# Neighbouring PSUM banks for a pair's products, and low parts subtracted by POOL, in a chunked attention with two feed-forward layers

## The chip, the cores and the metric

One Trainium2 chip, of which one core runs the whole program. The metric is the device time of one execution in microseconds. The engines of the core work side by side and each takes its own instructions in order: TensorE (PE for matmuls, PEld for loading weights), VectorE (DVE), ScalarE (ACT), GpSimd (POOL), and SyncE (SP), which here only issues DMAs.

## The reference

Attention in chunks of 64 tokens (4 batches, 8 heads, 576 tokens, head size 64), then two feed-forward layers over the 2304 tokens, with 512 features and 2048 hidden units, all in float32.

```python
scores = scale * np.matmul(q_c, k_c.transpose(0, 1, 2, 4, 3))       # chunks of 64 x 64
attn = softmax(scores)                                              # with 1e-09 in the sum
x = np.matmul(attn, v_c)                                            # -> [2304, 512]
h = x @ moe_w_in;   x = (h - np.tanh(h)) @ moe_w_out
h = x @ moe2_w_in;  x = (h * np.tanh(np.log1p(np.exp(h)))) @ moe2_w_out
```

The second activation is Mish.

## The kernel before

**Split numbers.** Every operand of a large matmul is kept as two rounded halves, a high part (ScalarE copies it with rounding) and a low part (the number minus its high part, a subtraction on VectorE). A product takes three matmuls: high by high, high by low, low by high (`THREE`). The helper `sub` (L80) issues the subtractions, so they all carry line 81, and `add` line 84.

**Layer 1** runs in 80 steps (`steps`): five blocks of tokens (512, 256, 512, 512, 512) by 16 units of 128 hidden features. Step s does `gemm1(s)` (12 matmuls into bank 4 or 5, `hidden`), the activation in pieces on ScalarE and VectorE (`gap_act`, `gap_mid`, `gap_poly`, and a step later `gap_end`), the high part (`hi_part`, ScalarE) and low part (`lo_part`, VectorE) of step s-1, and `gemm2(s-2)` (12 matmuls into banks 0 to 3). After a block's last unit `evacuate` copies banks 0 to 3 out and stores them in DRAM as the input of layer 2. The order in which everything is issued is written out by hand in the loop over `s`.

**Jobs inside layer 1.** From step 35 on, 16 jobs prepare the weights of layer 2, eight of w_in and eight of w_out, spread over the steps by the lists `job` and `cast`. A job loads, unpacks (`j_low`, `j_float`) and forms seven sums of quarter matrices (`j_sums`) in a tile `jf` that has two buffers. For w_out `j_split` makes the halves, `js`: ScalarE writes the high part, ScalarE writes the negated numbers, and a DMA issued by POOL adds the numbers to them (L194 to L200). `j_store` then writes both halves to DRAM; every `js` tile has one buffer. When all jobs are done (step `ends`) their memory is given to layer 2, and the first token pair is loaded (`x_load`), summed (`x_sums`, VectorE) and split (`x_split`, high parts on ScalarE, low parts on VectorE) in the next steps.

**Layer 2** works on three pairs of token blocks (2 x 384 tokens). It uses a scheme with seven products in place of eight quarter products for both matrix multiplications.

- `group1(p, jj)` is the first one, four groups for each pair of token blocks. A group has two neighbouring units, j0 = 2jj and j1 = 2jj+1. `both(p, jj, n)` issues product n (0 to 6) of j1 and then of j0, six matmuls each. Product n goes to bank `BANK1[n]` for j0 and four banks further for j1. Products 4, 5 and 6 go on accumulating in the banks of 0, 2 and 3. `bank1(n)` (L583) is the pair of banks n and n+4, read by one instruction: a copy by ScalarE (L597), sums by VectorE (L84, `u2`, `u3`, `g`), Mish by ScalarE (L587). At a group's end VectorE forms three more sums of `g`.
- The weights of a group come as two parts (`wf_load` on SP's queue, `wf_hi` on ScalarE, `wf_lo` on VectorE), for j1 and j0 each: part 0 for products 0 to 3, part 1 for 4 to 6. `wf_lo` issues the next load into the buffer that it has read. Part 1 has a single buffer for j1 and j0.
- `phase2(p)` is the second one: 56 slots of six matmuls, whose operand `g_split` prepares three slots ahead. Its results lie in neighbouring banks (`bank2`). At the same time the tokens of the next pair are loaded, summed and split.

For the first group the four products 0 to 3 of unit 1 are computed ahead, between layer 1's last gemm1 and its last gemm2s, into banks 4 to 7; those of unit 0 follow when `evacuate` has emptied banks 0 to 3.

Of the kernel before, what the change touches and what calls it, by code (L numbers as in the profile page):

```python
# [46 lines left out]
def attn_moe_moe(ctx, tc, qkv, w1, w2, out):  # L47
# [32 lines left out]
    def sub(o, a, b):  # L80
        nc.vector.tensor_tensor(o, a, b, op=ALU.subtract)  # L81
# [112 lines left out]
    def j_split(n, part):  # L194
        t = JF[n] if part == 0 else JF.pop(n)
        m, src = (4, t[:, 4:]) if part == 0 else (3, t[:, :3])
        o = (SA, SB)[part][n] = pools["j"].tile([P, 2, m, 2 * P], F32R, tag=f"s{part}", name="js", bufs=1)
        nc.scalar.copy(o[:, 0], src)
        nc.scalar.activation(o[:, 1], src, AF.Copy, scale=-1.0)
        nc.gpsimd.dma_start(out=o[:, 1].bitcast(F32), in_=src, accum_op=ALU.add)  # L200
# [193 lines left out]
    def lo_part(s):  # L394
        t = BLOCKS[steps[s][0]]
        sub(GO[s][:, 1, :t], GF.pop(s), GO[s][:, 0, :t].bitcast(F32))
# [87 lines left out]
    for i, n in enumerate(ORD):  # L484
        s = first_job + JOBS[i]
        at(cast, s, (j_turned, n))
        at(job, s, (j_low, n))
        at(job, s + 1, (j_float, n))
        if i + 2 < 2 * NJ:
            at(job, s + 1, (j_load, ORD[i + 2]))  # L490
        at(job, s + 2, (j_sums, n))
        ends = max(ends, s + 3)
        if n >= NJ:
            at(cast, s + 3, (j_split, n, 0))
            at(cast, s + 4, (j_split, n, 1))
            at(job, s + 5, (j_store, n, 0))
            at(job, s + 6, (j_store, n, 1))
            ends = max(ends, s + 6)
# [21 lines left out]
    def x_split(c, part, n):  # L520
# [9 lines left out]
        else:  # L530
            sub(lo, src, hi.bitcast(F32))
# [10 lines left out]
    def wf_load(p, j, part):  # L542
        m, src = ((4, slice(0, 4)), (3, slice(4, 7)))[part]
        pool = pools["x"] if part == 0 and j % 2 else pools["f"]
# [8 lines left out]
    def wf_lo(p, j, part):  # L553
        t = W2[p, j, part]
        sub(t[:, 1], WF.pop((p, j, part)), t[:, 0].bitcast(F32))
        if part == 0 and j + 2 < NJ:
# [9 lines left out]
    BANK1 = (2, 3, 0, 1, 2, 0, 1)  # L566

    def product1(p, j, n):
        a, c = ORDER[n]
        ps = banks[:, BANK1[n] + 4 * (j % 2), :TH]  # L570
# [12 lines left out]
    def bank1(n):  # L583
        return banks[:, n:8:4, :TH]
# [4 lines left out]
    def group1(p, jj):  # L589
        j1, j0 = 2 * jj + 1, 2 * jj  # L590
        g = G[p, jj] = pools["g"].tile([P, 7, 2, TH], F32, tag=f"g{jj}", name=f"g{jj}")
        if p + jj:
            both(p, jj, 0)
        else:
            product1(p, j0, 0)
        u2, u3 = out_tile(), out_tile()
        nc.scalar.copy(u2, bank1(2))  # L597
        if p + jj:
            both(p, jj, 1)
        else:  # L600
            product1(p, j0, 1)
        wf_hi(p, j0, 1)
        add(u2, u2, bank1(3))
        wf_lo(p, j0, 1)
        if p + jj:
            both(p, jj, 2)
        else:
            product1(p, j0, 2)
        add(u3, u2, bank1(0))
        if p + jj:  # L610
            both(p, jj, 3)
        else:
            product1(p, j0, 3)
        W2.pop((p, j0, 0))
        W2.pop((p, j1, 0))
        add(g[:, 3], u3, bank1(1))
        if jj == NJ // 2 - 1:
            w2_load(p, 0)
            w2_load(p, 1)
            mish(g[:, 3], g[:, 3])  # L620
            for k in range(AHEAD - 1):
                g_split(p, k)
        else:
            wf_hi(p, j1 + 2, 0)
            mish(g[:, 3], g[:, 3])
# [4 lines left out]
        mish(g[:, 0], bank1(2))  # L630
        both(p, jj, 5)
        add(g[:, 1], u2, bank1(0))
        mish(g[:, 1], g[:, 1])
# [8 lines left out]
        add(g[:, 2], u2, bank1(1))  # L642
# [3 lines left out]
        add(g[:, 4], g[:, 1], g[:, 3])  # L646
        sub(g[:, 5:7], g[:, 1:5:3], g[:, 0:1].to_broadcast([P, 2, 2, TH]))
        sub(g[:, 1], g[:, 2], g[:, 6])
# [9 lines left out]
    def g_split(p, k):  # L658
        q, j = divmod(k, NJ)
        src = G[p, j // 2][:, (0, 6, 5, 4, 2, 3, 1)[q], j % 2]  # L660
# [78 lines left out]
    for s in range(NS):  # L739
# [40 lines left out]
        if ends + 2 <= s < ends + 6:  # L780
            x_split(s - ends - 2, 0, 0)
            x_split(s - ends - 2, 1, 0)
        if s == NS - 1:
            wf_hi(0, 1, 0)
# [19 lines left out]
        if 0 <= c < 5:  # L804
# [5 lines left out]
            if c < 4:  # L810
                x_sums(c)
    assert not streamed and not job and not cast and ends + 5 < NS
    nc.scalar.preload_act_table_set("mish")

    wf_lo(0, 1, 0)
# [3 lines left out]
    for n in range(4):  # L819
        product1(0, 1, n)  # L820
# [9 lines left out]
    wf_load(0, 0, 0)  # L830
    wf_load(0, 1, 1)
    wf_hi(0, 0, 0)
    wf_lo(0, 0, 0)
# [57 lines left out]
```

## Time and profile before

| | before |
|---|---|
| median of 3 runs | 947.79 us (946.19 to 950.15) |
| the profiled execution | 952.0 us |
| its span, first to last instruction | 950.2 us |
| TensorE matmul / weight load busy | 850.5 / 736.6 us |
| VectorE / ScalarE / POOL busy | 666.6 / 516.4 / 23.2 us |
| mean granted clock of TensorE | 0.966 |

Times in the trace are microseconds from the span's start; 1.8 us of the profiled execution lie outside the span. L575 are the matmuls of `group1`, L674 those of `phase2`, L320 and L329 those of layer 1. "Idle before" is the time in which the engine stood still ahead of an instruction, with what ended it. Layer 1 ends near 514 us; `group1` fills 518 to 605, 664 to 746 and 805 to 886 us, `phase2` the stretches between and the end.

### The profile page before, as it was taken

How to read it: one execution, taken by the hardware profiler on the slowest of the kernel's cores; microseconds unless marked ns; L12 is line 12 of the kernel's file. 1: busy time of each engine (PE TensorE's matmuls, PEld its weight loads, DVE VectorE, ACT ScalarE, POOL GpSimd, SP SyncE). 2: the span in 40 equal slices, each digit the busy share in tenths (PEclk: the TensorE clock that was granted, in tenths of full speed). 3: DMA queues.
4: the chain of work that ended last, by engine and by line, in shares of the span. 5: the costliest groups of instructions: out<-in, count | busy, mean ns of one | idle time of the engine just before them, and what ended most of it. 6: DMA issues, size and time to landing. Idle time of an engine off the chain costs nothing.

```text
span 950.2 us, 13624 instructions
## 1 busy us (share of the span) xinstructions
PE 850.5 (90%) x5244; PEld 736.6 (78%) x5244; DVE 666.6 (70%) x1048; ACT 516.4 (54%) x867; POOL 23.2 (2%) x32
## 2 busy tenths in 40 slices
PE   7889989998899899989895788899888899888898
PEld 6667779976677777767664777899777799777897
DVE  7999758768697889668482555587555686555664
ACT  4888746657557667566353333465333465333443
POOL 0011100000000000000000000000000000000000
PEclk9999999999999999989997799999989999999999
DMA  9945736446898989797813321788221887231774
GB/s 379 419 154 122 166 125 207 158 156 227 290 359 218 348 313 327 229 296 200 281 35 121 100 81 35 270 287 296 95 79 37 290 288 277 94 94 55 250 264 136
DMA packets 60081, 193.83 MB, mean 204 GB/s; under 512 B 4848, under 2 KB 33008, under 8 KB 46832
## 3 DMA queue, kind: packets, MB, share of 16 engines
q1 hardware_dynamic: 56272, 180.37, 54.2%
q0 software_dynamic: 3744, 12.58, 7.1%
q8 instruction: 41, 0.67, 0.3%
q14 instruction: 24, 0.20, 0.1%
HBM read 140.51 MB, written 39.85 MB: 190 GB/s over the span
## 4 chain that ended last, share of the span: by engine, by line
PE 47%; DVE 24%; DMA 13%; ACT 10%; issue 5%; SPq 1%; DVEq 0%; ACTq 0%; POOLq 0%
PE banks L674 17%; PE banks L575 14%; PE banks L329 7%; PE banks L320 7%; DMA wf<-win 3%; DVE g L84 3%; DMA js<-jf 3%; DMA wout<-js 2%; DVE g L365 2%; DVE g L366 2%; DVE w L81 2%; DMA w<-wf 1%; DVE o L84 1%; DVE g L378 1%; DVE t L81 1%
## 5 line engine op out<-in xcount | busy, mean ns | idle before, releaser
L575 PE MATMUL banks<-xo,w 128*128 128x384 f32 x1008 | 212.3, 364 | 48.9 <-DVE o L84 20.5
L575 PEld LDWEIGHTS banks<-xo,w 128*128 128x128 f32 x1008 | 187.0, 203 | 74.2 <-DVE o L84 28.3
L329 PE MATMUL banks<-go,w 128*128 128x512 f32 (+1 forms) x960 | 225.9, 384 | 15.6 <-ACT go L392 5.6
L320 PE MATMUL banks<-x,w 128*128 128x512 f32 (+1 forms) x960 | 216.6, 374 | 7.1 <-DVE w L81 2.6
L329 PEld LDWEIGHTS banks<-go,w 128*128 128x128 f32 x960 | 171.5, 194 | 54.0 <-DVE go L81 7.6
L320 PEld LDWEIGHTS banks<-x,w 128*128 128x128 f32 x960 | 168.4, 189 | 43.4 <-DVE w L81 3.9
L674 PE MATMUL banks<-s,w 128*128 128x384 f32 x1008 | 176.4, 337 | 5.0 <-DVE g L84 3.1
L674 PEld LDWEIGHTS banks<-s,w 128*128 128x128 f32 x1008 | 174.5, 188 | 6.9 <-DVE g L84 4.1
L81 DVE TENSOR_TENSOR s<-g,s 128x384 fp32r<-128x384 f32 x168 | 87.2, 554 | 39.3 <-ACT s L662 39.1
L662 ACT CAST s<-g 128x384 fp32r<-128x384 f32 x168 | 81.7, 511 | 45.1 <-PE banks L674 43.9
L551 ACT CAST w<-wf 128x1024 fp32r<-128x1024 f32 (+1 forms) x48 | 44.7, 934 | 71.2 <-PE banks L575 41.7
L392 ACT CAST go<-g 128x512 fp32r<-128x512 f32 (+1 forms) x80 | 46.2, 578 | 67.4 <-DVE g L366 67.4
L587 ACT ACTIVATE g<-g 128x768 f32<-128x768 f32 x36 | 30.5, 847 | 92.3 <-DVE g L84 92.3
L378 DVE TENSOR_TENSOR g<-z,banks 128x512 f32<-128x512 f32 (+1 forms) x80 | 50.2, 627 | 40.5 <-ACT t L373 40.3
L84 DVE TENSOR_TENSOR g<-o,banks 128x768 f32<-128x768 f32 x36 | 34.4, 954 | 61.9 <-PE banks L575 61.9
L84 DVE TENSOR_TENSOR o<-o,banks 128x768 f32<-128x768 f32 x39 | 37.1, 952 | 54.0 <-PE banks L575 41.2
L81 DVE TENSOR_TENSOR w<-wf,w 128x1024 fp32r<-128x1024 f32 (+1 forms) x54 | 59.4, 1102 | 19.1 <-ACT w L551 18.6
L372 ACT ACTIVATE z<-banks 128x512 f32<-128x512 f32 (+1 forms) x80 | 43.9, 548 | 42.4 <-PE banks L320 42.3
L366 DVE COPY_PREDICATED g<-m,t 128x512 f32<-128x512 int16 (+1 forms) x80 | 55.1, 688 | 2.8
L81 DVE TENSOR_TENSOR go<-g,go 128x512 fp32r<-128x512 f32 (+1 forms) x80 | 50.4, 630 | 4.1 <-ACT go L392 4.1
L365 DVE SCALAR_TENSOR_TENSOR g<-z,g 128x512 f32<-128x512 f32 (+1 forms) x80 | 50.6, 633 | 2.8 <-ACT z L384 2.7
L81 DVE TENSOR_TENSOR t<-banks,t 128x512 f32<-128x512 f32 (+1 forms) x80 | 50.5, 631 | 0.0
(59 smaller groups left out, 663.1 us busy)
## 6 DMA issues: line engine op xcount, KB each, us to landing
w<-wout SPq DMA_DIRECT2D x42, 1024.0 KB, 5.6
w<-w1s SPq DMA_DIRECT2D x21, 1024.0 KB, 7.6
w<-w SPq DMA_DIRECT2D x16, 1024.0 KB, 19.9
jraw<-w SPq DMA_DIRECT2D x16, 1024.0 KB, 7.0
qkv<-qkv SPq DMA_DIRECT2D x18, 768.0 KB, 6.7
wf<-win SPq DMA_DIRECT2D x24, 512.0 KB, 3.8
wf<-win SPq DMA_DIRECT2D x24, 384.0 KB, 3.1
w1s<-w SPq DMA_DIRECT2D x8, 1024.0 KB, 8.8
```

Source lines behind the costliest of these rows:

```text
L81: nc.vector.tensor_tensor(o, a, b, op=ALU.subtract)
L84: nc.vector.tensor_tensor(o, a, b, op=ALU.add)
L320: nc.tensor.matmul(ps, w[:, a, k * P:(k + 1) * P], x[:, c, k, :BLOCKS[b]], start=n == 0, stop=n == 3 * KD - 1)
L329: nc.tensor.matmul(banks[:, m, :t], w[:, a, DM + m * P:DM + (m + 1) * P], g[:, c, :t], start=f == 0 and n == 0, stop=f == NF - 1 and n == 2)
L365: nc.vector.scalar_tensor_tensor(g, z, PK, g, op0=ALU.add, op1=ALU.mult)
L366: nc.vector.copy_predicated(g, m.bitcast(I16), t)
L378: nc.vector.tensor_tensor(g, z, ph, op=ALU.mult)
L392: nc.scalar.copy(o[:, 0, :BLOCKS[steps[s][0]]], GF[s])
L551: nc.scalar.copy(t[:, 0], WF[p, j, part])
L575: nc.tensor.matmul(ps, w[:, x, c % 4, k * P:(k + 1) * P], XO[p][:, a, y, k], start=m == 0 and n < 4, stop=m == 5, skip_group_check=n > 3)
L662: nc.scalar.copy(t[:, 0], src)
L674: nc.tensor.matmul(ps[:, m], w[:, x, j % 4, m * P:(m + 1) * P], s[:, y], start=n == 0 and j == 0 and q < 4, stop=n == 2 and j == NJ - 1, s ...
```

## The change

- **Banks.** `BANK1` is renumbered, and the two units of a pair write neighbouring banks: products 0 and 4 use banks 6 and 7, product 1 banks 4 and 5, products 2 and 5 banks 0 and 1, products 3 and 6 banks 2 and 3. `bank1(n)` is now `banks[:, b:b + 2]`. Two of the rows of `g` change places, so that one sum reads neighbouring rows.
- **Start of layer 2.** Instead of products 0 to 3 of unit 1, products 0 and 1 of both units are computed ahead. For that the first part of unit 0's weights is loaded and converted during layer 1 (step 79), after that of unit 1, which moves two steps ahead (step 77); it uses another pool. The loads for units 2 and 3 move behind that of unit 1's second part.
- **POOL.** `sub` takes an engine, and POOL now subtracts the low parts of layer 1's activation from step 32 on, of all tokens of layer 2 (`x_split`), of the second weight parts (`wf_lo`, part 1), and of the w_out sums. The latter replaces the negated copy on ScalarE and the accumulating DMA.
- **Stores.** `j_store` comes one step earlier, and so does all that follows step `ends`.

```diff
@@ -77,8 +77,8 @@ sub
-    def sub(o, a, b):
-        nc.vector.tensor_tensor(o, a, b, op=ALU.subtract)
+    def sub(o, a, b, eng=None):
+        (eng or nc.vector).tensor_tensor(o, a, b, op=ALU.subtract)
@@ -196,8 +196,7 @@ j_split
-        nc.scalar.activation(o[:, 1], src, AF.Copy, scale=-1.0)
-        nc.gpsimd.dma_start(out=o[:, 1].bitcast(F32), in_=src, accum_op=ALU.add)
+        sub(o[:, 1], src, o[:, 0].bitcast(F32), nc.gpsimd)
@@ -393,7 +392,7 @@ lo_part
-        sub(GO[s][:, 1, :t], GF.pop(s), GO[s][:, 0, :t].bitcast(F32))
+        sub(GO[s][:, 1, :t], GF.pop(s), GO[s][:, 0, :t].bitcast(F32), nc.gpsimd if s >= 2 * NF else nc.vector)
@@ -493,9 +492,9 @@ plan of the jobs
-            at(job, s + 5, (j_store, n, 0))
-            at(job, s + 6, (j_store, n, 1))
-            ends = max(ends, s + 6)
+            at(job, s + 4, (j_store, n, 0))
+            at(job, s + 5, (j_store, n, 1))
+            ends = max(ends, s + 5)
@@ -528,7 +527,7 @@ x_split
-            sub(lo, src, hi.bitcast(F32))
+            sub(lo, src, hi.bitcast(F32), nc.gpsimd)
@@ -541,7 +540,7 @@ wf_load
-        pool = pools["x"] if part == 0 and j % 2 else pools["f"]
+        pool = pools["x"] if part == 0 and (j % 2 or p + j == 0) else pools["f"]
@@ -552,8 +551,11 @@ wf_lo
-        sub(t[:, 1], WF.pop((p, j, part)), t[:, 0].bitcast(F32))
-        if part == 0 and j + 2 < NJ:
+        sub(t[:, 1], WF.pop((p, j, part)), t[:, 0].bitcast(F32), nc.gpsimd if part else nc.vector)
+        if p + j // 2 == 0 and part == 0:
+            if j:
+                wf_load(0, 0, 0)
+        elif part == 0 and j + 2 < NJ:
@@ -563,11 +565,11 @@ product1
-    BANK1 = (2, 3, 0, 1, 2, 0, 1)
+    BANK1 = (6, 4, 0, 2, 6, 0, 2)
...
-        ps = banks[:, BANK1[n] + 4 * (j % 2), :TH]
+        ps = banks[:, BANK1[n] + j % 2, :TH]
@@ -581,7 +583,7 @@ bank1
-        return banks[:, n:8:4, :TH]
+        return banks[:, BANK1[n]:BANK1[n] + 2, :TH]
@@ -589,48 +591,38 @@ group1
+        u2, u3 = out_tile(), out_tile()
...
-        else:
-            product1(p, j0, 0)
-        u2, u3 = out_tile(), out_tile()
-        nc.scalar.copy(u2, bank1(2))
+        nc.scalar.copy(u2, bank1(0))
...
-        else:
-            product1(p, j0, 1)
...
-        add(u2, u2, bank1(3))
+        add(u2, u2, bank1(1))
...
-        if p + jj:
-            both(p, jj, 2)
-        else:
-            product1(p, j0, 2)
-        add(u3, u2, bank1(0))
-        if p + jj:
-            both(p, jj, 3)
-        else:
-            product1(p, j0, 3)
+        both(p, jj, 2)
+        add(u3, u2, bank1(2))
+        both(p, jj, 3)
...
-        add(g[:, 3], u3, bank1(1))
+        add(g[:, 1], u3, bank1(3))
...
-            mish(g[:, 3], g[:, 3])
+            mish(g[:, 1], g[:, 1])
...
-            mish(g[:, 3], g[:, 3])
+            mish(g[:, 1], g[:, 1])
...
-        mish(g[:, 0], bank1(2))
+        mish(g[:, 0], bank1(4))
...
-        add(g[:, 1], u2, bank1(0))
-        mish(g[:, 1], g[:, 1])
+        add(g[:, 3], u2, bank1(5))
+        mish(g[:, 3], g[:, 3])
@@ -639,13 +631,13 @@ group1
-        add(g[:, 2], u2, bank1(1))
+        add(g[:, 2], u2, bank1(6))
...
-        add(g[:, 4], g[:, 1], g[:, 3])
-        sub(g[:, 5:7], g[:, 1:5:3], g[:, 0:1].to_broadcast([P, 2, 2, TH]))
-        sub(g[:, 1], g[:, 2], g[:, 6])
+        add(g[:, 4], g[:, 3], g[:, 1])
+        sub(g[:, 5:7], g[:, 3:5], g[:, 0:1].to_broadcast([P, 2, 2, TH]))
+        sub(g[:, 3], g[:, 2], g[:, 6])
@@ -657,7 +649,7 @@ g_split
-        src = G[p, j // 2][:, (0, 6, 5, 4, 2, 3, 1)[q], j % 2]
+        src = G[p, j // 2][:, (0, 6, 5, 4, 2, 1, 3)[q], j % 2]
@@ -780,8 +772,11 @@ loop over steps
+        if s == NS - 3:
+            wf_hi(0, 1, 0)
...
-            wf_hi(0, 1, 0)
+            W.pop(NF - 5)
+            wf_hi(0, 0, 0)
@@ -809,15 +804,17 @@ loop over steps
+        if s == NS - 3:
+            wf_lo(0, 1, 0)
...
-    wf_lo(0, 1, 0)
+    wf_lo(0, 0, 0)
...
-    for n in range(4):
-        product1(0, 1, n)
+    for n in range(2):
+        both(0, 0, n)
@@ -827,10 +824,9 @@ start of layer 2
-    wf_load(0, 0, 0)
...
-    wf_hi(0, 0, 0)
-    wf_lo(0, 0, 0)
+    wf_load(0, 3, 0)
+    wf_load(0, 2, 0)
```

## Rows read from the trace of the kernel before

**Rows 1.** The page, part 1: busy time of each engine
```profile
PE 850.5 (90%) x5244; PEld 736.6 (78%) x5244; DVE 666.6 (70%) x1048; ACT 516.4 (54%) x867; POOL 23.2 (2%) x32
```

**Rows 2.** Windows: busy us (and count) of each engine by stage, clock, DMA
```profile
181.60:285.64 104.04, 97.32 (x671) 78.16 (x669) 80.88 (x135) 63.78 (x111) 3.44 (x4) 0.98 0.72 248
285.64:387.50 101.86, 97.13 (x658) 77.23 (x656) 85.18 (x139) 70.79 (x116) 6.03 (x7) 1.00 0.89 285
387.50:502.77 115.27, 97.80 (x387) 75.96 (x385) 79.44 (x132) 67.23 (x111) 4.30 (x5) 0.93 0.67 210
...
664.27:746.30 82.03, 68.67 (x337) 60.30 (x336) 45.22 (x47) 27.93 (x35) 0.00 (x0) 0.96 0.28 91
...
605.03:664.10 59.07, 58.45 (x335) 58.13 (x336) 46.95 (x87) 35.46 (x67) 0.00 (x0) 1.00 0.86 301
```

**Rows 3.** Chain of waits: start, us, what; one stretch of `phase2`
```profile
609.22 55.22 PE banks L674 x317
```

**Rows 4.** Timeline of one `group1` group: start, us, engine, line, [idle before <-releaser]
```profile
555.80 0.80 ACT L587 ACTIVATE g<-banks 128x768 f32<-128x768 f32 x1
556.66 3.10 PEld L575 LDWEIGHTS banks<-xo,w 128*128 128x128 f32 x18 [1.47 <-ACT g L587]
...
559.14 0.95 DVE L84 TENSOR_TENSOR g<-o,banks 128x768 f32<-128x768 f32 x1 [1.99 <-PE banks L575]
...
560.15 2.03 PEld L575 LDWEIGHTS banks<-xo,w 128*128 128x128 f32 x12 [0.39 <-DVE g L84]
...
561.50 0.95 DVE L84 TENSOR_TENSOR g<-o,banks 128x768 f32<-128x768 f32 x1 [1.40 <-PE banks L575]
...
562.51 2.05 PEld L575 LDWEIGHTS banks<-xo,w 128*128 128x128 f32 x12 [0.32 <-DVE g L84]
...
564.23 2.82 DVE L81 TENSOR_TENSOR g<-g 128x1536 f32<-128x1536 f32 x2
...
566.97 0.95 DVE L84 TENSOR_TENSOR o<-o,banks 128x768 f32<-128x768 f32 x1
...
567.97 2.06 PEld L575 LDWEIGHTS banks<-xo,w 128*128 128x128 f32 x12 [2.24 <-DVE o L84]
```

**Rows 5.** Timeline of the same group: second weight part
```profile
562.37 0.95 DVE L81 TENSOR_TENSOR w<-wf,w 128x768 fp32r<-128x768 f32 x1
...
566.44 0.83 ACT L551 CAST w<-wf 128x768 fp32r<-128x768 f32 x1 [1.77 <-DMA wf<-win]
```

**Rows 6.** Timeline: turn from `group1` to `phase2`
```profile
604.02 0.95 DVE L84 TENSOR_TENSOR g<-o,banks 128x768 f32<-128x768 f32 x1 [1.41 <-PE banks L575]
...
609.22 5.85 PEld L674 LDWEIGHTS banks<-s,w 128*128 128x128 f32 x34 [0.94 <-DVE s L81]
```

**Rows 7.** Timeline: start of layer 2
```profile
517.99 1.78 PEld L575 LDWEIGHTS banks<-xo,w 128*128 128x128 f32 x6 [4.50 <-ACT o L347]
...
523.33 0.80 ACT L597 COPY o<-banks 128x768 f32<-128x768 f32 x1 [4.89 <-DMA x<-o]
```

**Rows 8.** Layer 1: timeline of one step, then waits (total us, times, longest)
```profile
387.08 0.62 ACT L392 CAST go<-g 128x512 fp32r<-128x512 f32 x1 [1.10 <-DVE g L366]
...
388.13 0.68 DVE L81 TENSOR_TENSOR go<-g,go 128x512 fp32r<-128x512 f32 x1
...
390.24 2.88 PE L329 MATMUL banks<-go,w 128*128 128x512 f32 x12
...
DVE jf L112 <- DMA js<-jf: 12.9, 3, 5.6
...
DVE xt L84 <- issue: 8.6, 1, 8.6
```

**Rows 9.** Groups of instructions: busy us, mean ns, idle before
```profile
L81 DVE TENSOR_TENSOR w<-wf,w 128x1024 fp32r<-128x1024 f32 (+1 forms) x54 | 59.4, 1102 | 19.1 <-ACT w L551 18.6
...
masks.py:199 POOL TENSOR_SCALAR_AFFINE_SELECT ident<-ident 128x128 f32<-128x128 f32 x1 | 0.3, 287 | 0.1
...
L878 POOL MEMSET const-float32-0.0<- 128x1 f32 x1 | 0.1, 98 | 0.2 <-issue 0.2
```

## Prediction

> **What bounds the kernel now.** I began with the page's busy shares [rows 1]: TensorE is 90% busy, no other engine above 70%, so the end can only move by what TensorE loses. The table by stage [rows 2] shows where. In layer 1's last 48 steps (181.6 to 502.8 us) it is idle for 6.7 + 4.7 + 17.5 = 28.9 us. The second product of layer 2 (`phase2`) loses almost nothing: 336 matmuls in 59.07 us, and its long undisturbed piece runs 317 in 55.22 us, 0.174 us each [rows 3]. The first product (`group1`, four groups of 84 matmuls, as many as `phase2` has) needs 82.0 us for the second pair of token blocks, where VectorE works 45 us and ScalarE 28. The same matmul count and shape costs 23 us more beside engines that are half idle: the loss is in waits.
>
> Which waits, the timeline of one group tells [rows 4]. Call the seven products b0 to b6, each 12 matmuls, the odd one of the pair (j1) first. b5 (banks 4 and 0) starts at 556.66, just when ScalarE's Mish of banks 2 and 6 ends (555.80 + 0.80), though b5's own banks were read long before. VectorE's read of banks 0 and 4 ends at 560.09, and at 560.15 b6 goes on in bank 1. Its read of 1 and 5 ends at 562.45, and at 562.51 b0 goes on in bank 2. Its read of 3 and 7 ends at 567.92, and at 567.97 b2 starts in bank 4. In every case the matmul goes to a bank that lies between the two that were read, never to one of them. So a pair read as `banks[:, n:8:4]` is guarded as the whole range from n to n+4. Each product waits for the reading of the one before it, and the last of these reads sits on VectorE behind 2.82 us of sums (564.23).
>
> **The change, part by part.**
>
> *Banks.* The pair becomes two neighbours; the range read is then exactly the two banks written, and the ranges of different products don't meet. What is left are true hazards. Let both(0) start at 0 and each product take 12 x 0.174 = 2.1 us. b4 needs the copy of b0 (done near 3, wanted at 8.4), b5 the sum of b2 (7.3, wanted at 10.5), b6 the sum of b3 (9.5, wanted at 12.5), the next b0 the Mish of b4 (12.2, wanted at 14.6). VectorE has seven sums of 0.95, a double one (2.82 - 0.95 = 1.9) and two weight low parts of about 1.1 [rows 4, 9]: 10.8 us of work in those 14.6. So a group falls to 84 x 0.174 = 14.6 us, if its weights come in time.
>
> The tightest chain is that of the second weight part, with one buffer. Today a low part ends at 563.32, the load of the other unit's part follows, and its conversion, 0.83 us, starts at 566.44, having waited for it [rows 5]: 3.1 us for the load. After: conversion ends 0.7 us behind b6, POOL's subtraction to 2.5, load 3.1 to 5.6, conversion to 6.5, POOL to 8.3; wanted at about 9.6. Cover 1.3 us.
>
> *The turn to `phase2`* changes less. Today VectorE's last sum starts at 604.02 and `phase2` stalls until its fourth slot's operand is there at 609.22 [rows 6]. The 5.2 us in between are VectorE's sums and one split; only three slots (3.1 us) are prepared. The wait for the last sum goes, but the fourth slot comes no earlier: the next wait is this one, about 2 us. From the start of its stage to the fourth slot of `phase2` the second pair took 82.0 + (609.22 - 605.03) = 86.2 us [rows 2, 6]; then 4 x 84 x 0.174 + 0.3 + 5.2 = 64. Gain 22; the third pair's stage looks the same, 21 to 22. The turn back to b0 is clean: `phase2` ends in banks 0 to 3, b0 is in 6 and 7.
>
> *Start of layer 2.* Now TensorE waits until 517.99 for the evacuation, which stands on ScalarE behind a weight load that can only be issued when gemm2(78) frees its room, and then for a copy at 523.33 that waits for the stores out of its buffer [rows 7]. After: j0's first weights are converted during layer 1, both b0 and b1 run there (24 matmuls as before). b2 starts some 2.3 us earlier, near 515.7: one conversion (0.83) fewer stands before the evacuation, four matmuls fewer stand ahead of gemm2(78) (about 0.9), and the load is now the first of its queue. The copy comes near 523.33 - 2.3 + 0.8 = 521.8, since the load issued behind POOL's 1.75 us subtraction (0.8 longer than VectorE's) stands before the stores on SP's queue. Copy and conversion end at 523.4, POOL's low part at 525.2, the rest of b4 with b5 and b6 (5.2) at 530.4. Three groups of 14.6 and 5.2 give the fourth slot at 579.4 instead of 609.22: gain 30. The moved steps: unit 1's conversion and low part go two steps ahead, where `x_split` has just been taken from VectorE; the load for unit 0 follows them on SP's queue, where nothing waits behind it until layer 1 ends; the loads for units 2 and 3 are wanted only a group later.
>
> *Subtractions on POOL.* No POOL subtraction is in the trace. From above: the affine select of 128x128 took 287 ns and a 128x1 memset 98 [rows 9], so 1.5 ns per element with one input; twice that for two inputs gives 1.6 us for 512, 2.35 for 768, 3.1 for 1024 elements. From below: VectorE's own 0.68 us for 512 [rows 8]. I take the middle, 1.2, 1.75 and 2.3, the select being the only row of that engine. VectorE gives away 48 x 0.68 = 33 us in layer 1, 24 x 0.95 = 23 in weights [rows 5] and the tokens, ScalarE the 16 negated copies.
> The Trainium skill (GPSIMD Engine Reference, section 3.1) has POOL at 4497 ns for 2048 elements of such an operation, 1.96 times VectorE; by that page a 512-element one is estimated at about 1.2 us, and no run here shows it yet.
>
> In layer 1 the low part of step s is wanted by gemm2 a step later: the conversion ended at 387.70, VectorE subtracted at 388.13, TensorE came at 390.24 [rows 8]. That leaves 2.5 us: 1.2 or 1.6 fit. On POOL's queue the w_out subtraction stands behind this step's low part and ahead of the next step's, 6.4 us later (101.86 / 16 [rows 2]); its wait for a free buffer is one ScalarE also makes. It is worth more than it looks: the accumulating DMA held the sums' buffer so long that VectorE stood 12.9 us in three waits, and TensorE behind it [rows 8]; a 2.3 us subtraction ends before the buffer is wanted, and the stores go one step earlier. On SP's queue they now stand ahead of the next step's reload of layer 1 weights; if POOL is late SP waits up to 2 us, but a reload is asked for four steps before its use. VectorE also does 0.7 us less per step where it is about 80% busy [rows 2], and less still in the last steps, which `x_split` fills. Not cured: the 8.6 us wait of x_sums [rows 8]; the stores, the loads and the sums all move by one step. Of the 28.9 us idle that leaves about 22; I take 18. Lower end -12 (the rival below), upper 28.
>
> In `phase2` TensorE is full; POOL gets eight token subtractions and a weight one (8 x 1.55 + 1.75 = 14 us in 59, with 1.55 as the mean of its two sizes), VectorE gets that much emptier: 0.
>
> **Sum:** 30 + 22 + 21 = 73 in layer 2, of which I leave 5 for waits of a few tenths at twelve group borders: 68. With 18: 86. The profiled execution took 952.0 us: 866. The median, 947.79, is 4.2 lower: **862 us**. At best 73 + 28 gives 847; 843 adds the 4 us by which the runs of before spread.
>
> **Rivals.**
>
> *Ports shared (880 to 893, chance 0.12).* POOL and VectorE may hinder each other in SBUF. The trace has no POOL subtraction, so nothing speaks for or against; if each POOL subtraction holds up VectorE's next two-input operation by up to its own 1.2 us, VectorE gains 0.7 and loses 1.2 in each of about 36 of the 48 steps, those in which it is short: 36 x 0.5 = 18 us, so layer 1's gain is 0 and the time 880; with the upper POOL price (1.6) another 36 x 0.4 = 14, of which I keep 12, since POOL waits at times itself: 892. Groups have 3.6 us of VectorE to spare and stay.
> The Trainium skill states just such a rule (SBUF — State Buffer, section Who interferes with whom): a VectorE instruction with two SBUF inputs and a POOL instruction that reads SBUF exclude each other, and the later one waits for the whole of the earlier. It speaks against this change; by it the time would be 880 to 892, and no row of the trace tests it.
>
> *The banks are not the cause (around 925, 0.08 with all between 893 and 943).* If the groups wait for something that ends at the same moments, only layer 1's 18 and a few us at the start are left: 947.8 - 22. Against it: four waits of four fit the range.
>
> *Slower (over 953, 0.03).* POOL becomes the bound of layer 1: a 512-element subtraction longer than the 2.5 us of cover delays gemm2 in each of 48 steps. All 86 us are eaten at 2.5 + 86 / 48 = 4.3 us, 2.7 times my upper price; at 4.6 the kernel is some 15 us slower than before, 962.
>
> **How the numbers follow.** Forecast, 843 to 880: 0.70. Better than 843: 0.05. Ports: 0.12. 893 to 943: 0.08. Within 0.5%, which is about what a measurement of this kernel can tell from no change: 0.02. Slower: 0.03. Range 843 to 893 (0.82). Faster 0.95.
>
> **What would show it.** Right: no matmul of `product1` waiting on a read of other banks; a group at 14.6 to 15.2 us; the stage of pair two at 59 to 61 instead of 82; a wait near 2 us before the fourth slot of each `phase2`; VectorE without waits for the sums' buffer; POOL's 512 rows at 0.85 to 1.6 us. Wrong: `product1` waiting for POOL's w (the weight chain too long), gemm2 waiting for POOL's go, VectorE's two-input rows of layer 1 longer than they are now, or a lower granted clock in the denser groups.

## The result and the profile after

The changed kernel takes 884.7 us (median of 4 runs, 882.8 to 885.7), the one before beside it 946.99: the ratio is 0.934 [0.931, 0.937]. That is 62 us gained where 86 were forecast: outside the forecast's own 843 to 880, inside the 880 to 893 of the rival with shared ports, and so inside the whole range, 843 to 893. The profiled execution took 882.8 us with a span of 881.0, against 952.0 and 950.2.

By stage, from the first matmul of one to the first matmul of the next, in the two profiled executions:

| stage | before | after | gain | forecast |
|---|---|---|---|---|
| layer 1, steps 32 to 79 | 309.2 | 307.8 | 1.3 | 18 |
| step 79 to the first `phase2` | 114.3 | 79.2 | 35.1 | 31 |
| `group1`, pair 2 | 82.1 | 58.2 | 23.8 | 23.5 |
| `group1`, pair 3 | 80.7 | 58.2 | 22.5 | 22 |
| `phase2`, pair 1 / 2 / 3 | 59.2 / 59.2 / 59.4 | 66.2 / 64.2 / 60.6 | -6.9 / -5.0 / -1.2 | -1.3 each |

(The prediction's 30, 22 and 21 went as far as the fourth slot of each `phase2`; here the longer stall ahead of that slot stands with `phase2`: the slot was forecast at 5.5 us from the start of `phase2` instead of 4.2, and came at 5.4.) The gains sum to 69.6; the spans differ by 69.2.

The page's first part of the kernel after, beside [rows 1]: TensorE's share rises, VectorE's busy time rises too, and POOL is busy eight times as long.

```profile
PE 816.8 (93%) x5244; PEld 723.5 (82%) x5244; DVE 673.2 (76%) x952; ACT 501.9 (57%) x851; POOL 192.6 (22%) x128
```

The windows of the kernel after, columns as in [rows 2] (PE, PEld, DVE, ACT, POOL, clock, DMA share, GB/s): steps 32 to 79, then `phase2` of pair 1, `group1` of pair 2 and of pair 3.

```profile
181.92:489.76 307.84, 283.52 (x1686) 223.45 (x1685) 245.99 (x340) 182.92 (x311) 106.00 (x69) 0.99 0.66 233
568.95:635.13 66.18, 61.22 (x337) 59.62 (x337) 51.09 (x79) 34.56 (x67) 15.42 (x9) 0.97 0.78 271
635.13:693.38 58.25, 58.25 (x338) 58.25 (x338) 42.35 (x38) 27.96 (x35) 12.93 (x7) 1.00 0.38 126
757.80:815.88 58.08, 58.08 (x337) 58.08 (x337) 42.35 (x38) 27.97 (x35) 12.94 (x7) 1.00 0.39 125
```

The same steps 32 to 79 of the kernel before:

```profile
181.60:490.78 309.18, 285.33 (x1686) 226.80 (x1685) 235.33 (x387) 193.75 (x324) 13.77 (x16) 0.97 0.79 256
```

`group1` is now without a gap. Layer 1 holds the surprise: VectorE has 47 instructions fewer, by about 0.68 us each [rows 8] some 32 us of work less, and is yet busy for 246.0 us instead of 235.3.

**`group1`** in the timeline of the kernel after (start, us, engine, [idle before <-releaser]), where [rows 4] had a wait at each product: one weight chain of the second part, and VectorE's sum beside it.

```profile
650.45 1.85 POOL L81 TENSOR_TENSOR w<-wf,w 128x768 fp32r<-128x768 f32 x1 [9.58 <-ACT w L550]
650.77 2.35 DVE L84 TENSOR_TENSOR g<-g 128x768 f32<-128x768 f32 x1
...
655.38 0.84 ACT L550 CAST w<-wf 128x768 fp32r<-128x768 f32 x1 [2.60 <-DMA wf<-win]
...
656.29 1.85 POOL L81 TENSOR_TENSOR w<-wf,w 128x768 fp32r<-128x768 f32 x1 [3.99 <-ACT w L550]
```

The chain is the one costed: POOL ends at 652.30, the load lands 3.1 us later at 655.38, and the second low part is there at 658.14, in time, since TensorE never waits in this stage. But VectorE's sum of 768 elements takes 2.35 us where 0.95 is its usual length: it ends at 653.12, 0.82 after POOL.

**The start of `phase2`**, beside [rows 6]:

```profile
693.57 0.95 DVE L84 TENSOR_TENSOR g<-o,banks 128x768 f32<-128x768 f32 x1 [1.13 <-PE banks L577]
...
698.78 5.33 PEld L666 LDWEIGHTS banks<-s,w 128*128 128x128 f32 x31 [2.21 <-DVE s L81]
```

From the last sum to the fourth slot it is 5.2 us, as before, and the wait there 2.21 instead of 0.94.

**Inside `phase2`** of pair 1, a piece that has no counterpart before:

```profile
583.95 1.61 POOL L81 TENSOR_TENSOR xo<-xs,xo 128x576 fp32r<-128x576 f32 x1 [21.06 <-ACT xo L528]
584.30 1.47 DVE L81 TENSOR_TENSOR xt<-xt,xs 128x192 f32<-128x192 f32 x1
...
587.26 1.84 POOL L81 TENSOR_TENSOR xo<-xt,xo 128x768 fp32r<-128x768 f32 x1 [1.70 <-ACT xo L528]
587.63 3.29 DVE L81 TENSOR_TENSOR s<-g,s 128x384 fp32r<-128x384 f32 x4 [0.85 <-ACT s L654]
589.57 1.51 PEld L666 LDWEIGHTS banks<-s,w 128*128 128x128 f32 x9 [1.21 <-DVE s L81]
```

A VectorE subtraction of 192 elements, 0.36 us elsewhere, runs from 584.30 to 585.77; POOL's subtraction ends at 585.56. Four subtractions of 0.56 take 3.29 us, because the first doesn't finish until POOL's has (589.10). Their result is the next operand of TensorE, which waits 1.2 us for it.

**In layer 1** the same, and once without harm:

```profile
341.84 1.29 POOL L81 TENSOR_TENSOR go<-g,go 128x512 fp32r<-128x512 f32 x1 [3.91 <-ACT go L391]
341.97 0.69 DVE L81 TENSOR_TENSOR t<-banks,t 128x512 f32<-128x512 f32 x1
...
352.91 2.40 POOL L81 TENSOR_TENSOR js<-jf,js 128x1024 fp32r<-128x1024 f32 x1 [0.84 <-ACT js L198]
352.98 3.42 DVE L112 SCALAR_TENSOR_TENSOR jf<-jraw 128x1024 int32<-128x1024 int32 x1
```

The unpacking (L112) takes 3.42 us where four of its kind with no POOL subtraction beside them take 1.22. The subtraction at 341.97, one of whose inputs lies in PSUM (`banks`), keeps its 0.69.

The groups of VectorE's instructions of the trace after that meet POOL's subtractions most, parted by whether one overlaps them (mean ns; counts in brackets):

| VectorE's instruction | inputs | alone | beside POOL | longest |
|---|---|---|---|---|
| `s<-g,s`, 384 | two, SBUF | 553 (154) | 1317 (14) | 1900 |
| `jf<-jraw`, 1024 | two, SBUF | 1216 (4) | 2264 (12) | 3417 |
| `jf<-jf`, 512 | two, SBUF | 682 (7) | 1554 (9) | 1569 |
| `jf<-jf`, 256 | two, SBUF | 425 (22) | 1185 (10) | 1956 |
| `g<-g`, 768 | two, SBUF | 953 (3) | 2383 (9) | 2645 |
| `g<-z,g`, 512 | two, SBUF | 683 (55) | 1602 (9) | 2891 |
| `g<-m,t`, 512 | two, SBUF | 747 (62) | 2828 (2) | 2835 |
| `t<-banks,t`, 512 | one in PSUM | 682 (17) | 684 (47) | 699 |
| `o<-o,banks`, 768 | one in PSUM | 951 (17) | 952 (22) | 955 |
| `rd<-e`, a reduction | one, SBUF | 676 (10) | 678 (8) | 692 |
| `jraw<-jraw`, 1024 | one, SBUF | 687 (14) | 1555 (2) | 1562 |

Summed over the instructions that are longer than alone, with the POOL subtraction that lies beside them: in layer 1 the w_out sums (`js`) hold VectorE up for 25.6 us, in 14 of its instructions, the activation's low parts (`go`) for 17.5, in 27; in layer 2 the tokens (`xo`) for 20.0 and the weights (`w`) for 12.9, these beside a `group1` in which TensorE waits for POOL once, 1.0 us in pair 1.

### The profile page after: what moved, and what is told of

It is laid out like the page before. It is cut to its first block, busy times and chain, and to the rows that moved or that the text cites. A ratio compares the mean times of both kernels' runs of the same rounds, so it can differ in the third digit from the quotient of the medians.

```text
span 881.0 us, 13693 instructions
## 1 busy us (share of the span) xinstructions
PE 816.8 (93%) x5244; PEld 723.5 (82%) x5244; DVE 673.2 (76%) x952; ACT 501.9 (57%) x851; POOL 192.6 (22%) x128
## 3 DMA queue, kind: packets, MB, share of 16 engines
q1 hardware_dynamic: 56272, 180.37, 58.2%
## 4 chain that ended last, share of the span: by engine, by line
PE 47%; DVE 33%; ACT 6%; DMA 6%; issue 5%; POOL 2%; SPq 1%; ACTq 0%; DVEq 0%; POOLq 0%
PE banks L577 19%; PE banks L666 16%; PE banks L328 6%; PE banks L319 5%; DVE g L364 4%; DVE jf L81 4%; DVE jf L112 3%; DVE g L365 3%; DVE g L377 2%; DVE t L81 2%; DVE s L81 2%; DMA w<-wf 2%; DVE wf L112 1%; POOL xo L81 1%; DMA x<-ev 1%
## 5 line engine op out<-in xcount | busy, mean ns | idle before, releaser
L328 PEld LDWEIGHTS banks<-go,w 128*128 128x128 f32 x960 | 168.7, 192 | 55.6 <-POOL go L81 10.1
L666 PE MATMUL banks<-s,w 128*128 128x384 f32 x1008 | 180.0, 339 | 11.4 <-DVE s L81 11.4
L577 PE MATMUL banks<-xo,w 128*128 128x384 f32 x1008 | 176.1, 334 | 4.7 <-ACT o L346 2.2
L577 PEld LDWEIGHTS banks<-xo,w 128*128 128x128 f32 x1008 | 174.9, 188 | 5.9 <-ACT o L346 2.6
L81 DVE TENSOR_TENSOR s<-g,s 128x384 fp32r<-128x384 f32 x168 | 96.6, 616 | 41.3 <-ACT s L654 41.0
L81 POOL TENSOR_TENSOR go<-g,go 128x512 fp32r<-128x512 f32 x48 | 61.9, 1290 | 264.4 <-ACT go L391 243.0
L81 POOL TENSOR_TENSOR w<-wf,w 128x768 fp32r<-128x768 f32 x24 | 44.3, 1846 | 155.1 <-ACT w L550 149.2
L364 DVE SCALAR_TENSOR_TENSOR g<-z,g 128x512 f32<-128x512 f32 (+1 forms) x80 | 58.8, 734 | 4.6 <-ACT z L383 4.6
L365 DVE COPY_PREDICATED g<-m,t 128x512 f32<-128x512 int16 (+1 forms) x80 | 59.2, 741 | 2.8
L383 ACT ACTIVATE z<-z 128x512 f32<-128x512 f32 (+1 forms) x80 | 47.2, 589 | 5.2 <-DVE g L377 2.8
```

The costliest lines, as they stand in the source:

```text
L81: (eng or nc.vector).tensor_tensor(o, a, b, op=ALU.subtract)
L328: nc.tensor.matmul(banks[:, m, :t], w[:, a, DM + m * P:DM + (m + 1) * P], g[:, c, :t], start=f == 0 and n == 0, stop=f == NF - 1 and n == 2)
L364: nc.vector.scalar_tensor_tensor(g, z, PK, g, op0=ALU.add, op1=ALU.mult)
L365: nc.vector.copy_predicated(g, m.bitcast(I16), t)
L383: nc.scalar.activation(z, z, AF.Square, scale=SQ_SCALE, bias=SQ_BIAS)
L577: nc.tensor.matmul(ps, w[:, x, c % 4, k * P:(k + 1) * P], XO[p][:, a, y, k], start=m == 0 and n < 4, stop=m == 5, skip_group_check=n > 3)
```

## The experiments

Ratios are to the kernel before on the same chip, taken beside it, with 95% intervals; stages are from one profiled execution each, in us. The same layer 1 stands in the kernel after, in e3 and in e7: 307.8, 308.5, 307.7, so a microsecond in that column says little. Where a `phase2` has a star its granted clock was 0.97, and its stall with the 30 matmuls behind it takes 8.9 us instead of 7.4 (last section); those at 1.00 are the ones to compare. The first `phase2` of e1 and of e12 is 1.0 us longer for another reason: behind the stall its matmuls come every 0.177 us instead of 0.173 with the granted clock at 1.00. Why isn't shown.

| kernel | ratio | steps 32 to 79 | step 79 to `phase2` | `group1` pairs 2, 3 | `phase2` pairs 1, 2, 3 |
|---|---|---|---|---|---|
| after | 0.934 | 307.8 | 79.2 | 58.2, 58.2 | 66.2*, 64.2, 60.6 |
| e1_banks | 0.926 [0.921, 0.931] | 311.0 | 82.0 | 58.2, 58.2 | 63.0*, 60.5, 62.2* |
| e2_pool | 1.005 [1.002, 1.007] | 307.4 | 107.3 | 79.8, 82.9 | 63.3, 63.0, 59.4 |
| e3_tokens_dve | 0.927 [0.922, 0.931] | 308.5 | 79.3 | 58.2, 58.2 | 60.5, 62.0*, 60.6 |
| e4_wout_dve | 0.934 [0.931, 0.938] | 310.9 | 79.2 | 58.2, 58.2 | 66.0*, 64.2, 60.6 |
| e5_writes_only | 0.896 [0.892, 0.899] | 284.0 | 76.0 | 58.2, 58.2 | 62.0*, 60.5, 62.2* |
| e6_lo_dve | 0.929 [0.927, 0.931] | 308.5 | 79.1 | 58.2, 58.2 | 66.0*, 64.2, 60.6 |
| e7_ahead | 0.917 [0.915, 0.919] | 307.7 | 79.0 | 58.2, 58.2 | 59.4, 59.4, 59.6 |
| e8_wout_writes | 0.915 [0.913, 0.917] | 296.7 | 77.5 | 58.2, 58.2 | 64.7, 64.2, 60.6 |
| e9_pieces | 0.907 [0.903, 0.910] | 301.7 | 79.0 | 58.2, 58.2 | 59.4, 59.4, 59.6 |
| e10_halves | 0.910 [0.907, 0.913] | 302.0 | 79.0 | 58.2, 58.2 | 59.4, 59.4, 59.6 |
| e11_pieces_lo_dve | 0.909 [0.905, 0.913] | 301.6 | 79.1 | 58.2, 58.2 | 59.4, 59.4, 59.6 |
| e12_wout_late | 0.919 [0.915, 0.925] | 311.3 | 77.7 | 58.2, 58.2 | 60.4, 59.4, 59.6 |

### The two halves of the change: e1 and e2

e1 is the kernel after with every subtraction back on VectorE and the w_out halves made as before:

```diff
-        sub(o[:, 1], src, o[:, 0].bitcast(F32), nc.gpsimd)
+        nc.scalar.activation(o[:, 1], src, AF.Copy, scale=-1.0)
+        nc.gpsimd.dma_start(out=o[:, 1].bitcast(F32), in_=src, accum_op=ALU.add)
```

> The bank numbering and the new start of layer 2 alone; all low parts are VectorE's again, w_out's sums go by negated copy and accumulating DMA, stores at their old steps. Theory (bank ranges were the waits of the first product; POOL's reads hold up VectorE's two-input operations and cost the gain in layer 1 and some 9.5 us in the second product): group1 stages 58 us for pairs two and three as in the changed kernel, each phase2 about 60.6 us instead of 66.4 and 64.4, layer 1 as before; so 947 - (35 + 23.8 + 22.5 - 3.6) = about 869 us, faster than the whole change. Rival (the longer phase2 belongs to the banks, since the stages before it now end earlier): phase2 stays at 64 to 66 us, about 879 us.

e2 is the kernel before with the POOL subtractions and the earlier stores alone (`BANK1` and the start of layer 2 untouched).

> POOL's subtractions and the earlier stores alone, on the old banks and the old start of layer 2. Theory: layer 1 gains about 1 us as in the whole change, group1 stays at 81 to 82 us, phase2 of pairs one and two loses 4 to 6 us each: 947 - 1 + 10 = about 956 us, slower. Rival (POOL is innocent of phase2's loss): phase2 stays at 59.4 us and the time at 946 us.

The banks and the new start alone give 879.7 us, the whole change 884.7. POOL's part alone gives 954.1 us against 950.7 beside it, 0.5% slower. So the first half by itself gives the whole gain and more; the second, for which the prediction had 18 us in layer 1, costs a few: by the ratios 0.0075 of 948 us, 7 us, with intervals that just touch. It does pay at the end of layer 1: from step 79 to gemm2(78) it is 17.4 us before and 17.5 in e1, 14.0 after and 12.2 in e2. e1 had been expected near 869 us: its layer 1 (311.0) and its start (82.0) are longer than was taken for them, and two of its `phase2` have a star. The windows of a `phase2` of e1, of the first of e2 and of the first of e3 show where:

```profile
698.72:759.34 60.62, 58.74 (x338) 58.41 (x338) 47.98 (x88) 35.34 (x67) 0.00 (x0) 1.00 0.85 301
```
```profile
597.83:661.27 63.44, 60.02 (x337) 58.41 (x338) 49.85 (x78) 34.89 (x67) 15.66 (x9) 1.00 0.79 276
```
```profile
571.04:631.66 60.62, 58.74 (x338) 58.41 (x338) 47.00 (x87) 35.34 (x67) 1.84 (x1) 1.00 0.85 296
```

With 78 instructions instead of 88 VectorE is busy for 49.85 us in e2 instead of 47.98.

### The tokens back on VectorE: e3

```diff
-            sub(lo, src, hi.bitcast(F32), nc.gpsimd)
+            sub(lo, src, hi.bitcast(F32), nc.vector if p else nc.gpsimd)
```

> The changed kernel with the token low parts of pairs two and three back on VectorE (those in phase2). Theory (ports): VectorE takes 2 x 6.8 us of subtractions back, yet phase2 falls from 66.4 and 64.4 to about 60.6 us: 885 - 9.5 = 875 us. Rival (VectorE's own load is phase2's limit, or the loss comes from the earlier start): phase2 stays or grows by up to 2 us: 885 to 889 us.

`phase2` falls to 60.5 at full clock, and the kernel to 879.5 us: eight subtractions of POOL, in a stretch where it is otherwise almost idle, had cost 3.7 us in pair 2 and about 4 in pair 1 (5.7 with the clock). What stays over 59.2 is the wait for the fourth slot. (875 us was expected; the starred pair 2 is 1.6 us of what is missing.)

### Does reading do the harm? e5 and e8

In e5 each POOL subtraction is replaced by two memsets of the same size (the low parts are zero, so the products leave out the high-by-low and low-by-high terms of what POOL made). POOL is occupied, but reads nothing:

```diff
+        if eng is nc.gpsimd:
+            for _ in range(2):
+                nc.gpsimd.memset(o.bitcast(F32), 0.0)
```

> The changed kernel with each of POOL's subtractions replaced by two memsets of the same tile: same queues, same waits, a similar time on POOL, but POOL reads nothing from SBUF. It leaves the low parts out (zeros stand in their place) wherever POOL made them. Theory (POOL's reads hold up VectorE's two-input operations): those operations are back at their lengths of before (jf<-jraw 1.2 us, s<-g,s 0.55 us); phase2 falls to about 60.6 us in all pairs, and steps 32 to 79 of layer 1, 307.8 us in the changed kernel, fall by 10 to 18 us, the gain that was forecast: about 860 us. Rival (layer 1 has another limit and would not have gained in any case): layer 1 stays at 306 to 309 us, only phase2 falls: 875 us.

Rows of the groups by line, after and then e5 (busy us, mean ns | idle before): the same VectorE instructions, with POOL reading and with POOL only writing.

```profile
L81 DVE TENSOR_TENSOR s<-g,s 128x384 fp32r<-128x384 f32 x168 | 96.6, 616 | 41.3 <-ACT s L654 41.0
L112 DVE SCALAR_TENSOR_TENSOR jf<-jraw 128x1024 int32<-128x1024 int32 x16 | 32.0, 2002 | 0.0
```
```profile
L85 DVE TENSOR_TENSOR s<-g,s 128x384 fp32r<-128x384 f32 x168 | 86.8, 555 | 47.9 <-ACT s L658 47.5
L116 DVE SCALAR_TENSOR_TENSOR jf<-jraw 128x1024 int32<-128x1024 int32 x16 | 19.5, 1217 | 0.0
...
L83 POOL MEMSET go<- 128x512 f32 x96 | 50.8, 529 | 267.6 <-PE banks L332 120.2 <-DVE t L85 66.8 <-ACT z L387 58.8
```

Both means are back at their length alone (553, 1216), and `phase2` is at 60.5. VectorE's busy time in steps 32 to 79 falls by 38.8 us to 207.2; the hold-ups summed there were 25.6 + 17.5 = 43.1, and busy time counts records that overlap only once. Layer 1 is 23.8 us shorter, more than expected. Not all of that is the hold-up: a memset waits for no high part, so gemm2's waits for POOL (5.7 us) and the tail's wait (below) change too.

e8 does the same for the w_out sums alone (their low parts are zero).

```diff
-        sub(o[:, 1], src, o[:, 0].bitcast(F32), nc.gpsimd)
+        for _ in range(2):
+            nc.gpsimd.memset(o[:, 1].bitcast(F32), 0.0)
```

> The changed kernel with only the 16 w_out subtractions replaced by two memsets each on POOL, so their low parts are left out; all else reads as in the changed kernel. Theory (ports): these 16 are two thirds of the 37 us by which VectorE is held up in layer 1, so steps 32 to 79 fall from 307.8 to between 293 and 300 us: 870 to 877 us. Rival (the hold-ups of layer 1 lie beside its limit): 306 to 309 us, 885 us.

Layer 1 falls by 11.1 us to 296.7, inside what was expected; 16 subtractions of 2.0 to 2.5 us did that. Here no product of layer 1 waits for what is left out, so this is the cleaner price: 11 us of end for 25.6 us of hold-up. (These memsets, too, wait for no high part; e9 below leaves the waits as they are.)

### Back to VectorE instead? e4, e6 and e12

e4 has the w_out subtraction on VectorE at the same place, e6 the activation's low part.

```diff
-        sub(o[:, 1], src, o[:, 0].bitcast(F32), nc.gpsimd)
+        sub(o[:, 1], src, o[:, 0].bitcast(F32))
```

> The changed kernel with the w_out low parts subtracted by VectorE instead of POOL (no accumulating DMA, stores at the new steps). Theory (ports): in the changed kernel's trace those 16 POOL subtractions stretch VectorE's operations by 24 us in layer 1; doing them on VectorE costs about 8 x 1.2 + 8 x 0.95 = 17 us; so layer 1 gains some 4 to 8 us: 877 to 881 us. Rival (VectorE's load, not the ports, keeps layer 1 from gaining): VectorE has 17 us more to do and layer 1 gets 5 to 12 us longer: 890 to 897 us.

```diff
-        sub(..., nc.gpsimd if s >= 2 * NF else nc.vector)
+        sub(...)
```

> The changed kernel with the low part of layer 1's activation back on VectorE in all steps; w_out, tokens and weights stay on POOL. Theory (ports, by the sums of the trace): VectorE takes 48 x 0.65 = 31 us back and is rid of some 12 us of being held up by these 48 subtractions: steps 32 to 79 get 5 to 15 us longer, 890 to 900 us. Rival (the hold-ups delay the activation's chain, VectorE's load doesn't count): 3 to 8 us shorter, 877 to 882 us.

e6: layer 1 is 308.5 us, the same as 307.8. I had expected 5 to 15 longer, and the rival's 3 to 8 shorter fell too. Giving these subtractions to POOL is worth nothing measurable: with 45 more of them in this stretch, 31 us at 0.68, VectorE is busy only 9.2 us longer (255.2), since the 17.5 us of hold-ups by `go` are gone, and that doesn't show at the end.

e4: layer 1 is 310.9, and the kernel as long as the change, between the 877 to 881 us expected and the rival's 890 to 897. The hold-ups by `js` are gone, but a row of VectorE's waits (total us, times, longest) has taken their place:

```profile
DVE js L81 <- ACT js L198: 25.2, 16, 1.7
```

VectorE takes its instructions in order and stands behind ScalarE's high part in each of the 16. e12 issues the subtraction later, at the end of the step, on top of e7:

```diff
+            at(job, s + 3, (j_lo, n, 0))
+            at(job, s + 4, (j_store, n, 0), (j_lo, n, 1))
```

> The run with four splits ahead, with the w_out subtractions on VectorE, but issued at the end of the step, well behind ScalarE's copy for which VectorE waited 25.2 us in e4_wout_dve. Theory (e4 only swapped 24 us of hold-ups for 25 us of waiting on ScalarE plus its own 17 us of work): without the waits layer 1's steps 32 to 79 fall from 310.9 in e4 to between 297 and 303 us: 858 to 865 us beside some 952 before, equal to or better than the pieces on POOL. Rival (17 us more work on VectorE cost as much as the hold-ups on POOL): 306 to 311 us, 871 to 876 us.

It still waits 17.1 us in 11 waits, and layer 1 takes 311.3, the kernel 872.0: what the rival had (306 to 311, 871 to 876), and not the 297 to 303 of the theory. But with the waits still there the run doesn't tell what the subtraction would cost VectorE without them; that stays open.

### A better version: e7, e9, e10, e11

e7 is e3 with the operands of `phase2` prepared one slot further ahead, in as many buffers as there were.

```diff
-AHEAD = 4
+AHEAD = 5
-    pools["s"] = ctx.enter_context(tc.tile_pool(name="ss", bufs=AHEAD + 1, reuse_waits="tile"))
+    pools["s"] = ctx.enter_context(tc.tile_pool(name="ss", bufs=AHEAD, reuse_waits="tile"))
```

> Token low parts of phase2 on VectorE, as in the run before with that edit (879.5 us beside 950.7 before), and four operand splits instead of three prepared ahead of phase2, in the same five buffers. Theory (the stall of about 2 us at phase2's start is VectorE's sums standing ahead of the fourth split): each phase2 falls from 60.6 to about 59.6 us, 3 us in all: 876 us beside 950.7. Rival (the stall has another cause or the buffers bind): no change, 879 us.

`phase2` takes 59.4 to 59.6 in all three pairs and the kernel 872.6 us: the longer wait for the fourth slot is gone, 1.0 us each time. By the medians e7 is 7 us shorter than e3, where 3 were expected; 1.6 of the rest is the star of e3, and what is left isn't accounted for.

e9 adds that POOL subtracts the w_out sums in pieces of 256 elements, so that it holds VectorE for a piece at a time; e10 also halves the activation's low parts; e11 is e9 with these on VectorE.

```diff
+        for q in range(m):
+            sub(o[:, 1, q], src[:, q], o[:, 0, q].bitcast(F32), nc.gpsimd)
```

> The run with four splits ahead (872.6 us beside 952.0 before), with each w_out subtraction on POOL issued as four or three pieces of 256 elements: the same work, 56 instructions for 16. Theory (an instruction of POOL keeps VectorE's two-input operations out until it ends, so short ones let VectorE in between): VectorE's longest hold-ups in layer 1 shrink from about 2.2 us to 0.7, and steps 32 to 79 fall from 307.7 to 298 to 304 us: 863 to 869 us. Rival (what counts is POOL's reading time in all): 307 to 309 us, 872 to 874 us.

> As e9_pieces, and each activation low part on POOL in two halves of 256 elements, 96 instructions for 48. Theory: the hold-ups by these, 12 us of VectorE in the changed kernel, shrink too: 1 to 4 us less than e9_pieces. Rival (a second fixed cost of about 0.13 us and the later end delay gemm2): the same or up to 3 us more than e9_pieces.

> As e9_pieces, with the activation's low part on VectorE in all steps. Theory: as in e6_lo_dve moving it back costs nothing as long as hold-ups set layer 1, but with the w_out hold-ups smaller VectorE's 31 us more begin to count: 2 to 8 us more than e9_pieces. Rival (the move to POOL is worth nothing here either): within 1 us of e9_pieces, or faster.

Groups of e9:

```profile
L81 POOL TENSOR_TENSOR js<-jf,js 128x256 fp32r<-128x256 f32 x56 | 54.8, 1006 | 9.7 <-ACT js L198 9.7
...
L112 DVE SCALAR_TENSOR_TENSOR jf<-jraw 128x1024 int32<-128x1024 int32 x16 | 27.4, 1711 | 0.0
```

POOL spends 54.8 us on what took 36.0, yet the unpacking falls from 2002 to 1711 ns, the hold-ups by `js` from 25.6 to 16.2 us (the longest from 2.2 to 0.54), and layer 1 by 6.0 against e7, as expected. POOL reads as much as before and waits for the same, so what shortens layer 1 is the length of each hold. e9 takes 863.7 us, 0.907 of before: the best version here that computes everything. Halving the low parts (e10) and taking them back (e11) gain nothing. By the ratios the three can't be told apart, but every run of e10 and e11 (865.27 to 867.71 and 863.89 to 866.92 us) is longer than every run of e9 (863.03 to 863.81); in the profiled executions, the shortest of e10 and e11, the stages agree within 0.4 us, so where these 2 to 4 us lie isn't shown.

## Why the prediction was right and wrong

**Banks: right.** Group and stage (58.2 us; 58.5 was worked out), no product waiting on a read of other banks, a weight chain with just enough cover: all as costed. e1 shows that this half gives the gain without the other. The 5 us left for small waits at group borders were not needed: in pairs 2 and 3 TensorE is never idle in `group1`.

**The next wait: right.** The fourth slot's operand came 5.2 us after the last sum and cost 1.2 us more than before; e7 takes it away.

**Start of layer 2: right, a little small.** 33.9 us net of the stall, against 30. The first matmuls behind the evacuation start at 511.66 instead of 517.99: 6.3 us earlier, of which layer 1 gives 1.0; I had 2.3. Of the 5.3 left, 3.4 are the shorter way to gemm2(78), which e1 doesn't have and which so belongs to POOL and the earlier steps. Behind them TensorE also runs faster. The windows from gemm2(78) to the second group, before and after, have a granted clock of 0.73 and 1.00:

```profile
508.20:540.14 31.94, 21.96 (x86) 18.90 (x86) 9.14 (x9) 9.98 (x14) 0.00 (x0) 0.73 0.43 136
```
```profile
503.76:525.27 21.51, 16.83 (x85) 14.78 (x85) 6.09 (x6) 8.36 (x12) 4.12 (x3) 1.00 0.54 178
```

As many matmuls of the same shapes are busy for 5.1 us less. The clock of this stretch goes with the start: 0.74 in e2, which has the old one, 0.92 to 1.00 in all runs with the new one. I had not put the clock into the sum.

**POOL's own lengths: right.** 1.29 us for 512 elements, 1.85 for 768 and 2.48 for 1024, where 1.2, 1.75 and 2.3 were taken.

**What POOL does to VectorE: wrong, and this is the miss of the profiled execution.** The step that failed is "VectorE also does 0.7 us less per step", with its twin "VectorE gets that much emptier: 0" for `phase2`. I counted what left VectorE and not what came back. Layer 1 gave 1.3 us for 18, `phase2` lost 9.2 us beyond its stall for 0 (some 1.6 of it clock), 26 us together; the 5 us of margin and the 4 of the start give some back, so that the profiled execution took 882.8 us where 866 was worked out. The other 6 us of the miss are the step from profile to median: before it was 4.2 down, after it is 1.9 up. Two of the signs that I had named as wrong are there: VectorE's two-input rows of layer 1 are longer, and gemm2 waits for POOL's `go` (5.7 us in seven waits of steps 32 to 79).

The rival had the mechanism and about the right time, but I gave it 0.12. Its price for layer 1, a hold-up of 1.2 us by `go` in 36 steps, 43 us, had in part the wrong culprit: `go` holds VectorE up for 17.5 us in all, since it often meets instructions that read PSUM (47 times `t<-banks,t`), and the fewer but longer w_out subtractions for 25.6. It also left out `phase2`, on the ground that the groups have VectorE to spare; but there each subtraction of VectorE is TensorE's next operand but three. That its 880 to 893 holds the measured time is so in part luck: 9.2 us that it left out stand against the margin and the longer gain at the start.

The Trainium skill (SBUF — State Buffer, section Who interferes with whom) says that a VectorE instruction with two SBUF inputs and a POOL instruction that reads SBUF exclude each other for the whole of the earlier one, and that in this POOL instructions which only write don't take part, nor VectorE's with one SBUF input outside its fast two-port modes. The trace agrees on each point: 553 becomes 1317 ns and 683 becomes 1602; with PSUM as an input 682 stays 684; beside memsets (e5) the mean is 1217, as alone. One input is no safe sign, though: `jraw<-jraw`, 1024 elements in 687 ns, takes 1555 beside a subtraction. I had quoted the rule and weighed it as unproven, since no row of before had a POOL subtraction. The absence of a row was no evidence against it.

**The accumulating DMA: right, and eaten.** VectorE's 12.9 us of waits for it [rows 8] are gone from the waits of after, and the hold-ups by `js`, 25.6 us, stand in their place.

**A wait that I missed.** The sums of the first tokens (`x_sums`) use a buffer `xt` that POOL must have read. POOL reads it last in the step, behind this step's `go` and the other token half. The tail of layer 1 after:

```profile
463.57 1.86 POOL L81 TENSOR_TENSOR xo<-xt,xo 128x768 fp32r<-128x768 f32 x1
...
465.47 0.36 DVE L84 TENSOR_TENSOR xt<-xs 128x192 f32<-128x192 f32 x1 [4.66 <-POOL xo L81]
```

VectorE stands 13.9 us in three such waits, and steps 72 to 79 take 50.1 us instead of 46.4. The prediction named what stands ahead on POOL's queue for `go` and `js`, and not for the tokens.

Whether VectorE, with a place found for it where ScalarE's half is ready, would make the w_out low parts more cheaply than POOL in pieces stays open (e12 didn't get there).

## What to carry to other kernels

An engine that takes work from another can give nothing where both read SBUF at the same time, as 48 subtractions did here (e6): cost the hold-up of the two-input instructions beside it, and move work to POOL where VectorE's instructions beside it read PSUM, or in short pieces, which was worth 6.0 us here. Where a matmul waits for a read of another bank, look whether a strided view of two banks spans those between. When an engine's queue is given a new tenant, list every tile with a single buffer that it now reads, and who writes that next.

## What the runs showed of the hardware that was not expected

- A VectorE instruction with both inputs in SBUF that meets a running POOL subtraction ends about its own length after POOL's end: 352.98 to 356.40 beside a subtraction to 355.31, own length 1.22. POOL is held in turn: its 768-element `js` takes 1.84 to 2.17 us, while the 768-element `w` takes 1.81 to 1.86.
- POOL's subtraction took at least 0.73, 1.27, 1.81 and 2.40 us for 256, 512, 768 and 1024 elements: 0.54 to 0.59 for each 256, and 0.2 on top.
- A memset on POOL took 529 ns for 512 elements and 741 for 768, and lengthened neither of the two VectorE groups of e5 shown above. Two groups with one input it did lengthen: `jraw<-jraw` (689 ns alone, up to 995) and `rd<-rd`, eight elements (171 alone, up to 984).
- The stall ahead of the fourth slot has a second price now and then. Windows of the first `phase2` after, and of the same piece of its second:

```profile
573.00:575.00 2.00, 0.65 (x3) 0.65 (x4) 2.00 (x4) 0.04 (x1) 0.00 (x0) 0.93 0.96 394
575.00:577.00 2.00, 2.00 (x8) 2.00 (x7) 1.56 (x4) 0.51 (x1) 0.00 (x0) 0.50 0.53 179
577.00:579.00 2.00, 2.00 (x10) 2.00 (x10) 0.64 (x2) 0.51 (x1) 0.00 (x0) 0.72 0.95 270
```
```profile
697.40:699.40 2.00, 0.62 (x3) 0.62 (x4) 2.00 (x4) 0.07 (x1) 0.00 (x0) 1.00 0.92 378
699.40:701.40 2.00, 2.00 (x14) 2.00 (x13) 1.67 (x4) 0.91 (x2) 0.00 (x0) 1.00 0.75 216
```

  The first time TensorE, idle for nearly 2 us, comes back at the lower level (0.50, 1.2 GHz) and does 8 and 10 matmuls in 2 us each instead of 13; the second time, after the same pause, it doesn't. Of the 21 `phase2` with the long stall (after, e1, e3 to e6, e8) eight show it, of the 21 of before, e2, e7 and e9 to e12 none. What decides between the two is open.
